# Batch 0's inverse on 32x32 blocks, its landmark sums made transposed, and a new order of all pieces, in a fused Nystrom-attention and SiLU-MLP kernel

## The chip, the cores and the metric

The kernel runs on one core of a Trainium2 chip. The metric is the device time of one execution in microseconds (us). Three runs of the kernel before gave 247.44, 250.91 and 253.49 us; the median, 250.91 us, is the time to compare with.

## The reference

Attention with landmarks (Nystromformer) over 8 batches of 8 heads, 576 tokens, head width 64, and then a two-layer network with SiLU on the joined heads. Per batch and head, with m = 32 landmarks that are means of 18 consecutive tokens:

```
q_lm, k_lm = means of 18 tokens                       # 32 x 64
A  = softmax(q k_lm^T / 8)      # 576 x 32
Bm = softmax(q_lm k_lm^T / 8)   # 32 x 32
C  = softmax(q_lm k^T / 8)      # 32 x 576
Z  = Bm^T / (norm1(Bm) * norminf(Bm))
six times: Z = 2 Z - Z Bm Z
attn = A Z C v                  # 576 x 64
out  = silu(x w_in) w_out       # x: 4608 x 512, w_in: 512 x 2048, w_out: 2048 x 512
```

All inputs and the output are float32; the kernel computes in bf16 and f16 with float32 sums.

## The kernel before

The work goes batch by batch, and the stages of neighbouring batches are interleaved. The eight heads of a batch are two groups g of four heads; a group's four 32-row blocks fill the 128 partitions. Per batch b:

- **Loads** (L360 to L425, queue of POOL, with the cast to bf16): `ld1.b` is k, `ld0.b` is q, `ldv0.b` to `ldv2.b` are v. Batch 0's q and k come as four halves (`ld00.0`, `ld01.0`, `ld11.0`, and the first half of k as float32 on SP's queue, `ldk`, cast on chip by `k0cACT` and `k0cDVE`). `wi..` are pieces of w_in, `wo..` of w_out. q and k lie in two buffers (batch b in buffer b mod 2), v too.
- **Transposes** of q and k: batches 0 to 2 on TensorE (`tr`, L512, evacuated by `trc`); batches 3 to 7 by four DMA transposes each on SP's queue (`xt10`, `xt11` for k, `xt00`, `xt01` for q, L539).
- **Landmark sums**: batches 0 and 1 on TensorE (`lms`, L555: 72 matmuls of 64 columns that add 18 slices each with the identity as weights; `lmc` copies the sums, `ltr`, L592, transposes them, `lmT` evacuates). From batch 2 on, a tree of additions on DVE (`lra` to `lrd`, L575), then `ltr` with the matrix `fold`, then `lmT`.
- **Bm and its inverse**: `sb` (L611), `pb` (exp), `pbs`, `pbr`, `bmx`, `csb`, `bmt`, `bbd`, `n1`, `nrm`, `f0`, `stz`, `stf`; then six steps. A step is `fb` (L683, a DVE product that spreads the 32x32 blocks of the weights into a block-diagonal 128x128 matrix), `ns` (L702, matmul) and `nsd` (L708, DVE: twice the state less the product). Batch 0 runs each group as a chain of its own (`ns00`, `ns01`, ...); the other batches run both groups together.
- **A, C and the rest**: `A`, `C` (matmuls), `Ax`, `Cx` (exp on ACT), `S`, `Ln`, `Rs`, `etn` (row sums and their division), `ct` (C transposed: `ctm` on TensorE for batches 0 and 1, a DMA transpose on SP at L814 after that), `cv` (C times v), `wc`, `zbd`, `zt`, and `m0` to `m3` (times w_in, evacuated by `mc`).
- **First layer** (L891): `h0` to `h15`, two matmuls of 512 columns each, and `hx`; ACT applies SiLU (`g`, `gx`).
- **Second layer**: `o` (plain products, the first ones) and from then on seven products `p1` to `p7` per pair of 128-row blocks, eight matmuls of 256 columns each, with sums on DVE (`ss`) and evacuations `c..`, `u2`; stores `os` on SP's queue, at the end on ACT's too.

`SEQUENCE` (L19) is one list of all these pieces, written out; each engine and each DMA queue runs its own pieces in the order of that list, and a piece starts when its operands are there. `*n` in it stands for n matmuls of 256 columns on zeros ("fillers", L442), which nothing reads. A name with `/ACT` or `/DVE` says which engine copies. Two rules add waits that the data don't ask for: a DMA transpose waits for one v load of its batch or of the next (`gate`, L539; L814), and the loads of a batch wait for the DMA transposes of an earlier one:

```
        gate = last[b - 1].get("xts", [])[-2:-1]
        if b - 2 >= NCT:
            gate = gate + last[b - 2]["cts"][:1]
        load_qk(b, 100.0 * b - 150, p["qk_read"], gate)
        load_v(b, 100.0 * b - 149, [p["cv"]], gate)
```

Of the kernel before, what the change touches and what calls it, by code (L numbers as in the profile page):

```python
# [19 lines left out]
ldk ld11.0 const ident k0cACT k0cDVE k0 *15 lms100.0 tr15.0 tr10.0 trc10.0/DVE lms106.0 lms1012.0  # L20
*6 lms110.0 lms116.0 tr114.0 lms1112.0 lmc1.0/DVE ld00.0 *6 lms000.0 tr05.0 tr00.0 trc05.0/ACT
trc114.0/ACT ltr1.0 lmT1.0/ACT trc00.0/DVE tr19.0 trc19.0/DVE trc15.0/DVE lms006.0 ld01.0
lms0012.0 lms010.0 lms016.0 lms0112.0 ld0.1 ld1.1 ldv2.0 ldv0.0 wi0b1 ldv1.0 wi0b0 tr09.0 tr014.0
lmc0.0/DVE *1 ltr0.0 lmT0.0/ACT *6 sb.0 pb.0 trc014.0/DVE trc09.0/DVE A.0 Ax01.0 Ax00.0 Ax10.0
Ax11.0 *5 C.0 Cx01.0 Cx10.0 Cx11.0 Cx00.0 pbs.0 pbr.0 bmx.0 bmt.0 csb.0 n1.0 nrm.0 tr09.1 lms000.1
lms006.1 S10.0 lms0012.1 lms010.1 bbd.0 trc09.1/DVE stz.0 f0.0 stf0.0 stf1.0 fb00.0 lms016.1
Ln10.0 S00.0 Ln00.0 fb01.0 lms0112.1 lmc0.1/DVE S01.0 ns00.0 nsd00.0 Ln01.0 S11.0 ns01.0 Ln11.0
nsd01.0 fb11.0 ctm00.0 ctc00.0/DVE tr05.1 trc05.1/ACT tr00.1 trc00.1/ACT Rs1.0 Rs0.0 ns11.0
nsd11.0 fb10.0 fb21.0 tr19.1 trc19.1/DVE ltr0.1 lms100.1 lms106.1 ns10.0 nsd10.0 lms1012.1 tr014.1
lms110.1 lms116.1 trc014.1/DVE ns21.0 tr114.1 lmT0.1/ACT wi1a wi0a wi1b1 wi1b0 wi3b0 wi3a  # L30
lms1112.1 lmc1.1/ACT tr10.1 trc10.1/ACT tr15.1 *2 ltr1.1 lmT1.1/ACT fb20.0 nsd21.0 etn1.0
trc15.1/DVE ns20.0 fb31.0 *3 ns31.0 ctm10.0 trc114.1/ACT etn0.0 nsd31.0 sb.1 pb.1 *1 A.1 Ax01.1
Ax00.1 nsd20.0 fb30.0 pbs.1 wrc.0 *1 ns30.0 nsd30.0 ctc10.0/DVE fb40.0 pbr.1 fb41.0 bmx.1 bmt.1
wi3b1 Ax11.1 Ax10.1 *5 C.1 Cx00.1 Cx11.1 Cx01.1 *1 ns40.0 nsd40.0 ns41.0 nsd41.0 fb50.0 fb51.0
cv0.0 cv1.0 wc.0 S01.1 Ln01.1 ns50.0 nsd50.0 *2 ns51.0 bbd.1 nsd51.0 zbd.0 S11.1 Ln11.1 S00.1
Ln00.1 wi2b0 wi2b1 wi2a ldv0.1 ldv1.1 *5 zt.0 ztc.0/DVE S10.1 ctm00.1 ctc00.1/DVE Rs0.1 Ln10.1
Cx10.1 *2 m1.0 mc11.0/ACT mc10.0/DVE m0.0 f0.1 mc01.0/DVE mc00.0/ACT *1 ctm10.1 ctc10.1/DVE Rs1.1
# [12 lines left out]
nrm.2 stz.2 o3@5000.0 hx8.1 f0.2 gx8.1 h0.1 g0.1 oc@5000.0/ACT h2.1 h10.1 g10.1 h4.1 h1.1 g2.1  # L50
g1.1 wt11 wt21 stf0.2 fb00.2 ns00.2 h13.1 g13.1 wt31 nsd00.2 fb10.2 wt10 wt20 wt30 p1@5020.0
c1@5020.0/ACT ns10.2 nsd10.2 fb20.2 h9.1 h6.1 g4.1 g9.1 g6.1 ss00@5100.0 p5@5020.0 c5@5020.0/DVE
hx0.1 gx0.1 ss10@5100.0 l1done.0 C.2 Cx00.2 Cx10.2 p6@5020.0 u2@5020.0/DVE ld1.3 ldv1.3 xt10.3
xt11.3 ns20.2 nsd20.2 ss20@5100.0 p3@5020.0 c12@5020.0 p7@5020.0 ld0.3 xt01.3 xt00.3 ldv0.2 ldv2.2
ldv1.2 l1done.1 A.2 Ax01.2 Cx11.2 ct1.2 Ax10.2 Ax11.2 p1@5100.0 c1@5100.0/ACT Ax00.2 Cx01.2 ct0.2
os@5000.0 ld1.4 lra1.3 fb30.2 ns30.2 p2@5020.0 ss30@5100.0 lrb1.3 os@5001.0 S10.2 S11.2 Ln11.2
Ln10.2 Rs1.2 p6@5100.0 S01.2 Ln01.2 S00.2 Ln00.2 p5@5100.0 nsd30.2 lrc1.3 fb40.2 lrd1.3 ltr1.3
c22@5020.0 lra0.3 u2@5100.0/DVE lrb0.3 p4@5020.0 ns40.2 lrc0.3 lrd0.3 ltr0.3 c11@5020.0 etn1.2
nsd40.2 c5@5100.0/ACT p3@5100.0 Rs0.2 lmT1.3/ACT etn0.2 lmT0.3/ACT sb.3 c12@5100.0 c21@5020.0/ACT
p7@5100.0 pb.3 pbs.3 pbr.3 fb50.2 A.3 Ax11.3 cv0.2 ldv1.4 c22@5100.0 wrc.2 wc.2 ld0.4 ldv0.3  # L60
ldv2.3 ldv2.4 ns50.2 nsd50.2 Ax10.3 Ax00.3 S11.3 Ln11.3 Ax01.3 p2@5100.0 C.3 Cx00.3 Cx01.3 Cx10.3
# [6 lines left out]
p4@5120.0 c21@5120.0/ACT nsd20.3 fb30.3 ns30.3 hx0.2 nsd30.3 fb40.3 h15.2 gx0.2 g15.2 ns40.3
nsd40.3 ct0.3 xt00.4 ld1.5 ldv0.4 h9.2 g9.2 g14.2 h1.2 h0.2 g1.2 g0.2 cv0.3 ldv1.5 fb50.3
ss30@5120.0 ns50.3 wc.3 nsd50.3 zbd.3 ld0.5 h11.2 g11.2 h13.2 g4.2 g13.2 h3.2 g3.2 etn1.3 zt.3  # L70
ztc.3/DVE etn0.3 p3@5120.0 c12@5120.0 m3.3 mc30.3/ACT m0.3 mc01.3/DVE mc00.3/ACT m2.3 mc21.3/ACT
m1.3 mc20.3/ACT h2.2 hx8.2 g2.2 h6.2 g6.2 mc31.3/DVE h12.3 gx8.2 h3.3 h10.3 mc10.3/DVE mc11.3/DVE
h7.3 h2.3 g2.3 h4.3 g4.3 g10.3 h13.3 h5.3 g5.3 hx8.3 gx8.3 g13.3 h9.3 h11.3 g7.3 h14.3 h6.3 g6.3
g11.3 p1@5200.0 g3.3 h8.3 g8.3 ss00@5200.0 p5@5200.0 hx0.3 g14.3 g9.3 ss00@5220.0 xt11.4 xt01.4
xt10.4 ss10@5200.0 lra1.4 lrb1.4 lrc1.4 ss10@5220.0 ss20@5220.0 lrd1.4 lra0.4 lrb0.4 os@5020.0
ss20@5200.0 l1done.2 ltr1.4 h1.3 h0.3 g0.3 g1.3 g12.3 h15.3 gx0.3 c1@5200.0/DVE p6@5200.0
u2@5200.0/ACT os@5021.0 ss30@5200.0 c5@5200.0/DVE p3@5200.0 ss30@5220.0 lmT1.4/DVE lrc0.4 lrd0.4
ltr0.4 lmT0.4/ACT g15.3 p1@5220.0 sb.4 pb.4 c1@5220.0/ACT xt11.5 xt10.5 c12@5200.0 lra1.5 lrb1.5
lrc1.5 p7@5200.0 c22@5200.0 lrd1.5 p2@5200.0 c11@5200.0 p4@5200.0 c21@5200.0/ACT C.4 Cx11.4 Cx10.4
Cx01.4 p6@5220.0 u2@5220.0/ACT Cx00.4 p5@5220.0 c5@5220.0/ACT A.4 Ax01.4 Ax10.4 Ax00.4 Ax11.4  # L80
pbs.4 pbr.4 bmx.4 xt01.5 xt00.5 lra0.5 csb.4 ss00@5300.0 p1@5300.0 S10.4 ltr1.5 p7@5220.0 lrb0.5
ss10@5300.0 ss20@5300.0 lrc0.5 n1.4 nrm.4 wrc.4 lrd0.5 ltr0.5 lmT0.5/ACT S00.4 p3@5220.0 l1done.3
os@5120.0 os@5121.0 Ln10.4 os@5200.0 ct0.4 ld0.6 stz.4 c1@5300.0/ACT bmt.4 lmT1.5/DVE bbd.4 f0.4
sb.5 pb.5 stf0.4 S11.4 Ln11.4 Rs1.4 p2@5220.0 S01.4 Ln01.4 fb00.4 ns00.4 c22@5220.0 pbs.5
c11@5220.0 c12@5220.0 Ln00.4 p5@5300.0 c5@5300.0/ACT Rs0.4 p4@5220.0 c21@5220.0/ACT pbr.5
# [96 lines left out]
class Plan:  # L182
# [14 lines left out]
    def run(self):  # L197
# [5 lines left out]
        seen = set()  # L203
# [41 lines left out]
def kernel(  # L245
# [9 lines left out]
    nc = tc.nc  # L255
# [907 lines left out]
```

## Time and profile before

| what | us |
|---|---|
| runs | 247.44, 250.91 (median), 253.49 |
| span of the profiled execution, first to last instruction | 245.4 |
| TensorE (PE) busy in it, fillers included | 233.3 |
| ACT, DVE, POOL busy | 180.8, 180.0, 36.7 |
| PE: first filler to first landmark sum | 1.13 to 5.00 |
| PE: longest idle stretch after that | 5.42 (98.75 to 104.17) |
| PE: granted clock of 0.50 | 101.54 to 108.37 |
| PE: last matmul ends | 241.0 |

The profiled execution's own time is its span and what lies around it; the page gives the span alone, which is 2.0 us below the fastest run and 5.5 below the median. A busy share is the union of an engine's instructions. Matmuls overlap, so the duration of one (193 ns for 64 columns) is longer than the distance to the next.

### The profile page before, as it was taken

What the parts mean: (1) busy time and instruction counts of PE and PEld (TensorE: products, weight loads), DVE (VectorE), ACT (ScalarE), POOL (GpSimd) and SP (SyncE); (2) the same over time, 40 slices, a digit from 0 to 9 for tenths busy, and PEclk for the clock granted to TensorE, in tenths of its full rate; (3) what the DMA queues carried; (4) which work ended last, traced back from release to release, by engine and by line L of the source; (5) the groups of instructions that cost most, each with busy time, mean ns of one, the idle gap of its engine ahead of it and who ended that gap; (6) DMA issues with size and microseconds to landing.
All of it is one profiled execution on the core that took longest, in us unless ns stands there. A gap on an engine that the chain in (4) does not pass through costs nothing.

```text
span 245.4 us, 7471 instructions
## 1 busy us (share of the span) xinstructions
PE 233.3 (95%) x2948; PEld 165.8 (68%) x2948; DVE 180.0 (73%) x503; ACT 180.8 (74%) x432; POOL 36.7 (15%) x62
## 2 busy tenths in 40 slices
PE   7999999999999999199999999999999999999992
PEld 5986464457867556067878754777876765789882
DVE  2589889789998591489798968938899475348752
ACT  3299999988989998159746699999779788634100
POOL 8346713000050040000130060000000000000000
PEclk9999999999999999769999999999999999999999
DMA  6999999999999999793999999985414421012343
GB/s 160 207 203 197 206 207 206 210 205 204 132 177 220 202 137 178 185 194 98 136 190 171 167 185 239 190 145 136 108 47 117 121 52 39 1 43 77 88 119 109
DMA packets 55876, 36.84 MB, mean 150 GB/s; under 512 B 36640, under 2 KB 47392, under 8 KB 55840
## 3 DMA queue, kind: packets, MB, share of 16 engines
q0 software_dynamic: 15120, 18.06, 45.1%
q1 hardware_dynamic: 39808, 17.35, 34.9%
q10 hardware_dynamic: 912, 0.95, 1.4%
q8 instruction: 23, 0.38, 0.6%
q14 instruction: 13, 0.11, 0.1%
HBM read 36.70 MB, written 9.44 MB: 188 GB/s over the span
## 4 chain that ended last, share of the span: by engine, by line
PE 78%; ACT 7%; DMA 7%; SPq 3%; issue 1%; DVE 1%; ACTq 0%; DVEq 0%
PE ps L325 74%; DMA qT<-qk 6%; PE ps L515 3%; SPq L539 2%; ACT gm L913 2%; DMA gm<-in_k_dram 1%; ACT L913 1%; SPq L814 1%; ACT L1116 1%; ACT gx L936 1%; ACT m L335 1%; PE ps L802 1%; DVE red L575 1%; ACT pb L641 1%; ACT et L742 0%
## 5 line engine op out<-in xcount | busy, mean ns | idle before, releaser
L913 ACT ACTIVATE gm<-ps 128x512 f16<-128x512 f32 x128 | 68.7, 621 | 15.0 <-PE ps L325 14.3
L325 PE MATMUL ps<-etn,m 128*128 128x512 bf16 (+1 forms) x512 | 73.5, 289 | 0.2
L325 PEld LDWEIGHTS <-gm 128*128 128x128 f16 x512 | 48.6, 98 | 12.5 <-issue 1.3
L325 PE MATMUL ps<-w_out_sb,gm 128*128 128x256 f16 (+1 forms) x392 | 53.0, 281 | 0.0
L325 PEld LDWEIGHTS <-ss 128*128 128x128 f16 x408 | 39.5, 99 | 9.8 <-issue 1.8
L325 PEld LDWEIGHTS <-m 128*128 128x128 bf16 x512 | 31.5, 98 | 20.8 <-issue 3.2
L325 PE MATMUL ps<-wt,ss 128*128 128x256 f16 x272 | 35.5, 276 | 0.2
L1036 DVE TENSOR_TENSOR ost<-ost,ps 128x256 f32<-128x256 f32 x51 | 20.9, 416 | 13.4 <-PE ps L325 7.4
L335 ACT COPY ost<-ps 128x256 f32<-128x256 f32 (+1 forms) x45 | 17.2, 388 | 10.9 <-PE ps L325 10.6
L335 ACT CAST m<-ps 128x512 bf16<-128x512 f32 x36 | 19.4, 612 | 1.1 <-PE ps L325 0.8
L337 DVE CAST m<-ps 128x512 bf16<-128x512 f32 x28 | 18.3, 685 | 2.3 <-PE ps L325 1.9
L710 DVE SCALAR_TENSOR_TENSOR st<-st,ps 128x128 bf16<-128x128 bf16 (+2 forms) x54 | 13.6, 257 | 8.5 <-PE ps L325 5.5
L407 POOL DMA_DIRECT2D v<-in_v_dram x24 | 14.0, 590 | 30.8 <-DMA qT<-qk 13.6
L325 PE MATMUL ps<-w_out_sb,ss 128*128 128x256 f16 x136 | 17.5, 273 | 0.0
L325 PE MATMUL ps<-wt,gm 128*128 128x256 f16 x120 | 15.5, 272 | 0.0
L575 DVE TENSOR_TENSOR red<-qT 128x1024 f16<-128x1024 bf16 x12 | 8.3, 689 | 9.4 <-DMA qT<-qk 9.2
L685 DVE TENSOR_TENSOR fb<-st,hmask 128x256 bf16<-128x256 bf16 (+1 forms) x54 | 14.4, 271 | 0.8
L752 ACT ACTIVATE ln<-ps 128x288 f32<-128x288 f32 x32 | 12.4, 423 | 2.7 <-PE ps L325 2.4
L787 ACT ACTIVATE ce<-ps 128x288 bf16<-128x288 f32 x32 | 13.0, 424 | 1.7 <-PE ps L325 1.6
L1001 DVE TENSOR_TENSOR ss<-gm 128x1024 f16<-128x1024 f16 x15 | 10.2, 686 | 5.2 <-ACT gm L913 5.2
L742 ACT ACTIVATE et<-ps 128x288 bf16<-128x288 f32 x32 | 11.1, 423 | 3.6 <-PE ps L325 3.6
L337 DVE COPY ost<-ps 128x256 f32<-128x256 f32 x25 | 10.5, 420 | 3.2 <-PE ps L325 3.0
(93 smaller groups left out, 332.0 us busy)
## 6 DMA issues: line engine op xcount, KB each, us to landing
out_dram<-ost SPq DMA_DIRECT2D x126, 64.0 KB, 2.1
v<-in_v_dram POOLq DMA_DIRECT2D x24, 192.0 KB, 10.0
qk<-in_q_dram POOLq DMA_DIRECT2D x7, 576.0 KB, 10.6
qk<-in_k_dram POOLq DMA_DIRECT2D x7, 576.0 KB, 9.2
w_out_sb<-in_moe_w_out_dram POOLq DMA_DIRECT2D x4, 512.0 KB, 15.1
w_in_sb<-in_moe_w_in_dram POOLq DMA_DIRECT2D x8, 128.0 KB, 7.2
w_in_sb<-in_moe_w_in_dram POOLq DMA_DIRECT2D x4, 256.0 KB, 9.0
out_dram<-ost ACTq DMA_DIRECT2D x10, 64.0 KB, 1.7
```

Of the source, the lines that this page charges most:

```text
L325: nc.tensor.matmul(out=out_ap, lhsT=lhsT, rhs=rhs, start=start, stop=stop, skip_group_check=True)
L335: nc.scalar.copy(out=out, in_=in_)
L337: nc.vector.tensor_copy(out=out, in_=in_)
L407: lambda e, a=a: nc.gpsimd.dma_start(out=v_r[b % 2][a * L:(a + 1) * L, :, :], in_=v[b].rearrange("h (l a x) d -> a l h (x d)", l=L, a=VA)[ ...
L575: lambda e: nc.vector.tensor_tensor(out=o_, in0=a_, in1=b_, op=OP.add),
L685: nc.vector.tensor_tensor(out=fb[it % 2][:, g0:g1], in0=bc(sr[it % 3][:, g0:g1, 0:L], 4, 2), in1=bc(hmask, n, 1), op=OP.mult), [o], 14.5 + ...
L710: nc.vector.scalar_tensor_tensor(out=s2[:, g0:g1, lo:SW], in0=s[:, g0:g1, lo:SW], scalar=2.0, in1=ps[:, 0:NG * SW].rearrange("p (g x) -> p ...
L742: lambda e, g=g, et=et, c=c: nc.scalar.activation(out=et[:, c], in_=bank(me["A"], 2 * g + c)[:, 0:HS], func=AF.Exp, scale=sc / J),
L752: lambda e, g=g, c=c, ln=ln: nc.scalar.activation(out=ln[:, c], in_=bank(me["S", g, c])[:, 0:HS], func=AF.Ln),
L787: nc.scalar.activation(out=ce[:, :, 0:VP].rearrange("p (i c) (a l) -> p c a i l", c=2, a=VA)[:, c], in_=bank(me["C"], 2 * g + c)[:, 0:HS]. ...
L913: lambda e, dc=dc, cell=cell: nc.scalar.activation(out=gm[:, dc, :], in_=bank(cell["o"]), func=AF.Silu),
L1036: nc.vector.tensor_tensor(out=out_, in0=x, in1=y, op=OP.add)
```

## The change

It does three things.

1. **Batch 0's landmark sums transposed.** The weights are now the 64 columns of a q or k slice and the moving operand is the 128-column identity, so the sum comes out transposed. It is made twice, into PSUM partitions 0 to 63 and 64 to 127, with two matmuls for each of the 72 slices: 144 matmuls of 128 columns in place of 72 of 64. `lmc` and `ltr` of batch 0 fall away; `lmT` reads the sums directly.
2. **Batch 0's inverse on compact blocks.** `ns` of batch 0 multiplies the 32x32 blocks as they lie, eight matmuls of 32 rows and 32 columns of weights per step (each block at its own quarter of rows and columns); `fb` falls away, and both groups run as one chain, like the other batches. 12 `ns`, 12 `nsd`, 12 `fb` and 2 `stf` become 6 `ns`, 6 `nsd` and 1 `stf`.
3. **A new `SEQUENCE`** for all pieces of all batches: 46 fillers in place of 64, and the waits between kinds of transfers are no longer made by rules but written in the list, as `name<other`: the piece waits until the transfer `other` has landed.

The core of the diff:

```
-            name, _, e = word.partition("/")
+            word, *gates = word.split("<")
+            name, _, e = word.partition("/")
             o = named.pop(name)
-            assert all(id(d) in seen for d, _ in o.deps), name
-            seen.add(id(o))
+            placed[name] = o
+            o.after = [placed[x] for x in gates]
...
-                    qt_ops[t, g][0].after = gate
...
                             for j in range(j0, j0 + 6):
+                                if cr:
+                                    for c in range(2):
+                                        mm(ps[Dh * c:Dh * c + Dh, g * 128:(g + 1) * 128],
+                                           qk[:, t, g, j, :], idb, start=(j == 0),
+                                           stop=(j == J - 1))
+                                    continue
                                 mm(ps[:, g * Dh:(g + 1) * Dh], idb, qk[:, t, g, j, :],
...
-        parts = [[0], [1]] if cr else [[0, 1]]
+        for gs in ([0, 1],):
...
                     for g in gs:
+                        if cr:
+                            for h in range(4):
+                                r = slice(L * h, L * h + L)
+                                mm(ps[r, g * SW + lo:(g + 1) * SW], s[r, g, 0:L], s[r, g, lo:SW])
+                            continue
                         mm(ps[:, g * SW + lo:(g + 1) * SW],
                            fb[it % 2][:, g].rearrange("p a l -> p (a l)"), s[:, g, lo:SW])
...
-                ct_ops[g][0].after = v_ops.get(b + 1, [])[-2:-1]
```

(`cr` is true for batch 0 alone.) The waits in the new list:

```
ld1.1<ldk ld0.1<ldk wi3a<ldk ldv1.0<ldk ldv0.0<ldk wi3b0<ldk ldv2.0<ldk
xt10.3<wo2 ldv1.3<xt11.3 ldv1.2<xt10.3 ldv2.2<xt01.3 xt00.3<ldv1.3 ct0.2<ldv1.2
ld1.4<os@5000.0 ldv2.3<ct1.2 ld1.5<xt11.4 ld0.5<xt10.4<os@5020.0 ldv1.5<xt00.5
ct1.4<ld0.7 ldv2.4<ct1.4 ldv1.4<ct1.4 ld0.6<os@5200.0 ld1.7<ct0.4 ldv2.7<xt00.6
ldv1.6<os@5341.0 ldv0.6<ct0.6 ldv1.7<ct0.6
```

The DMA pieces around batch 4's transposes, in the two lists (other pieces left out):

```
before: ct1.2 ct0.2 os@5000.0 ld1.4 os@5001.0 ldv1.4 ld0.4 ldv0.3 ldv2.3 ldv2.4 os@5100.0
        os@5101.0 ct1.3 ct0.3 xt00.4 ld1.5 ldv0.4 ldv1.5 ld0.5 xt11.4 xt01.4 xt10.4 os@5020.0
after:  ct1.2 os@5000.0 ldv0.2 ct0.2 ld1.4 os@5001.0 ldv2.3 ldv0.3 ld0.4 xt11.4 os@5021.0 ld1.5
        ct1.3 ct0.3 xt00.4 os@5020.0 xt10.4 xt01.4 os@5100.0 ld0.5 xt10.5 os@5121.0 xt11.5 xt00.5
        ldv1.5 xt01.5 ld0.7 os@5120.0 os@5101.0 ld1.6 os@5201.0 ct1.4 ldv2.4 ldv0.4 ldv1.4
```

Before the first `lms` the list has 15 fillers before and 8 after; from there to the first `h` 48 and 33; behind that 1 and 5. The loads of batch 0 start with q in the new list (`ld00.0 ld01.0`, then `ld11.0`), with k before.

More of the change, by code (lines that the diff above doesn't have):

```diff
@@ L19 @@
 SEQUENCE = """
[L20 to L25, printed above, removed]
@@ L32 @@
[L32 to L37, printed above, removed]
@@ L50 @@
[L50 to L61, printed above, removed]
@@ L68 @@
[L68 to L79, printed above, removed]
@@ L80 @@
[L80 to L85, printed above, removed]
@@ new lines @@
+trc15.2/ACT tr19.2 etn1.1 tr10.2 ns40.1 trc19.2/ACT trc10.2/DVE nsd40.1 *1 etn0.1 h14.0 g14.0 h8.0
+fb50.1 h5.0 g5.0 h13.0 tr114.2 h0.0 trc114.2/DVE lra1.2 lrb1.2 wrc.1 h4.0 l1done.3 g10.0 g3.0 g0.0
+g4.0 *1 ns50.1 nsd50.1 hx8.0 ld1.3 xt11.3 xt10.3<wo2 lrc1.2 zbd.1 gx8.0 lrd1.2 tr05.2 g13.0 g8.0
+trc05.2/DVE hx0.0 tr014.2 cv0.1 wc.1 tr00.2 wo3 ltr1.2 lmT1.2/ACT ld0.3 trc014.2/DVE zt.1 tr09.2
+ztc.1/ACT trc00.2/DVE h12.0 gx0.0 trc09.2/DVE g12.0 m3.1 mc30.1/ACT m2.1 m1.1 lra0.2 o0@5001.0
+mc20.1/DVE mc31.1/DVE lrb0.2 mc21.1/ACT o0@5000.0 h8.1 mc11.1/ACT lrc0.2 mc10.1/ACT h4.1 g4.1
@@ new lines @@
+S10.5 nsd50.4 wc.4 S11.5 zbd.4 Rs0.5 ct0.5 zt.4 c1@5340.0/ACT ztc.4/ACT xt10.6 ct1.5 c22@5320.0
+Ln10.5 xt11.6 nsd20.5 c12@5320.0 p4@5320.0 xt01.6 fb30.5 ns30.5 os@5301.0 Ln11.5 c21@5320.0/ACT
+nsd30.5 m1.4 m0.4 mc11.4/DVE m3.4 mc30.4/DVE p2@5340.0 p5@5340.0 mc31.4/ACT c11@5340.0 fb40.5
+ns40.5 xt00.6 Rs1.5 etn0.5 h14.4 mc00.4/DVE ss30@5340.0 mc10.4/ACT h7.4 g7.4 ss10@5340.0
+ld1.7<ct0.4 p6@5340.0 nsd40.5 fb50.5 c5@5340.0/ACT m2.4 p3@5340.0 mc21.4/ACT ns50.5 os@5321.0
+mc01.4/ACT u2@5340.0/DVE mc20.4/DVE g14.4 c12@5340.0 nsd50.5 ldv2.5 cv0.5 h15.4 g15.4 h12.4 h9.4
```

244 lines of the change are left out of this document (136 added, 108 removed).

## Prediction

> **What bounds the kernel now.** I read the page first, then the chain of waits, busy time by windows, and the timeline of the stretches that these name.
>
> ```profile
> span 245.4 us, 7471 instructions
> PE 233.3 (95%) x2948; PEld 165.8 (68%) x2948; DVE 180.0 (73%) x503; ACT 180.8 (74%) x432; POOL 36.7 (15%) x62
> PE   7999999999999999199999999999999999999992
> PEclk9999999999999999769999999999999999999999
> ```
>
> TensorE works all the time but for three places: the start, one hole at 40% of the span, where its clock falls too, and the end. The windows price them (columns: length, then busy time of PE, PEld, DVE, ACT, POOL, then granted clock, DMA share, GB/s).
>
> ```profile
> 1.13:5.00 3.87, 3.38 (x15) 2.25 (x16) 1.17 (x9) 1.68 (x2) 3.59 (x7) 1.00 0.70 194
> 31.25:98.75 67.50, 67.29 (x855) 42.64 (x853) 52.76 (x142) 62.73 (x143) 10.06 (x16) 1.00 1.15 189
> 98.75:104.17 5.42, 0.00 (x1) 0.00 (x1) 2.83 (x7) 0.44 (x1) 0.00 (x0) 0.76 0.74 182
> 104.17:108.40 4.23, 4.23 (x15) 2.10 (x16) 4.16 (x10) 2.06 (x4) 0.00 (x0) 0.51 1.07 201
> 108.40:241.00 132.60, 132.15 (x1566) 99.46 (x1563) 97.93 (x260) 93.24 (x227) 7.43 (x12) 1.00 0.60 119
> 241.00:245.40 4.40, 0.00 (x0) 0.00 (x0) 0.42 (x1) 0.00 (x0) 0.00 (x0) 0.94 0.30 81
> ```
>
> Outside the hole PE waits 0.21 us of 67.50 and 0.45 of 132.60. The chain (start, length, what) says what the hole is:
>
> ```profile
> 80.56 3.22 SPq L539
> ...
> 86.72 14.41 DMA qT<-qk
> ...
> 101.23 0.70 DVE red L575
> ...
> 104.17 15.06 PE ps L325 x139
> ```
>
> A DMA transpose of batch 4 is issued at 86.72 and lands 14.41 us later; the median of this kind is 4.2 (page, part 6). The sum tree on DVE and PE's `ltr1.4` wait for it. POOL shows what ran beside it:
>
> ```profile
> 86.34 0.71 POOL L400 DMA_DIRECT2D qk<-in_k_dram  x1 [13.68 <-issue]
> 87.04 1.16 POOL L407 DMA_DIRECT2D v<-in_v_dram  x2
> 88.20 0.71 POOL L400 DMA_DIRECT2D qk<-in_q_dram  x1
> ```
>
> The next batch's loads went out around that transpose. The start, in the timeline (start, length, instructions):
>
> ```profile
> 1.13 3.38 PE L325 MATMUL ps<-zer 128*128 128x256 bf16 x15 [1.13 <-DVE zer L434]
> 5.29 0.98 PE L515 MATMUL ps<-idb,qk 128*128 128x128 bf16 x9
> 6.46 0.82 PE L325 MATMUL ps<-zer 128*128 128x256 bf16 x6
> 8.69 0.67 PE L515 MATMUL ps<-idb,qk 128*128 128x128 bf16 x9
> 22.69 0.55 PE L325 MATMUL ps<-v,ct 96*32 96x64 bf16 x48
> ```
>
> Fifteen fillers take 0.21 us each, six later ones 0.11; nine transposes 0.98, later 0.67: PE is at half pace until about 6.2, though the clock column says 1.00 there.
>
> **The change, term by term**, against the span of 245.4.
>
> *The hole: -7.5.* It costs 5.42 idle, and then 4.23 us of work at clock 0.51, so 2.1 more. In the new list `xt11.4` no longer stands behind `ct1.3` and `ct0.3`, these two lose their wait for `ldv1.4`, and of the next batch's loads only `ld1.5` may run beside the last three transposes (`ld0.5` waits for `xt10.4`; `ldv1.5` for `xt00.5`). Between `xt01.4` and `ltr1.4` lie, in PE's order, 23 pieces `h`, 4 `hx`, 5 products and 5 `m`, about 18 us at 0.43 (42.74 to 43.17 in the timeline), 0.45, 0.87 (97.25 to 98.12) and 0.35; before, the last three transposes stood right ahead of their tree. Even the slowest landing, 14.4, then ends before `ltr1.4`. Bounds: 0 (the hole stays) to -7.5. I take -7.5, since what made the row of 14.41 late, two q/k loads and two v loads at once, is pulled apart.
>
> *Fillers: -1.2.* From the first landmark sum on 38 are left of 49, at 0.108. The first 15 becoming 8 gains nothing: PE waits for `ldk` either way (5.00).
>
> *`lmc`, `ltr` of batch 0: -0.2.* Four matmuls at 0.056 (nine transposes: 0.67 less one latency of 0.22, by 8). The two copies, 0.42 each, lie beside fillers and transposes; without these they would be 0.8 of path.
>
> *Landmark sums: +1.6.* Before, 72 at 0.034 (12 in 0.51), 2.4. After, 144 of 128 columns: 4.0 if the two halves overlap (72 x 0.056), 8.1 if not; so +1.6 to +5.7. I take +1.6, by the nearest row: 48 matmuls on column tiles in 0.55, or 8 ns each.
>
> *Newton steps: 0 on the path beyond the fillers.* DVE loses 12 `fb` (216 ns) and 12 `nsd` (212, two of 180), gains 6 of 283: 3.4 us less in a stretch, 12 to 27, where it is busy 13.16 of 14.95. The old chain runs from 15.51 (first `ns`) to 24.25 (`zbd`), 1.46 per step; a new step is 0.20 + 0.28 + two hand-overs of 0.1, 0.7, so 4.5 us less for six. But PE's order decides: between `sb.0` and `zt.0` it holds about as much other work as before, pulled up from batch 1. Bounds: -4.5 (the chain sets the start of `h`) to 0; I take 0, since PE idles 0.04 us there.
>
> *Tile changes: +1.4.* Sixteen 64x32 matmuls of `m` at 25.47 take 0.56 until the next piece starts, eight at 27.49 take 0.35: 0.026 each and 0.14 fixed. Ten new changes (6 `ns`, 4 groups of sums) cost 0 to 2.8 (in and out); I take one each, 1.4. The Trainium skill, TensorEngine Tiling (Array Packing), Key Properties, says that a change of the tiling mode drains TensorE; by it all changes in and out would pay, 2.8, and the sum would be 1.4 higher. The 0.14 agrees with it.
>
> *Clock at the start: +0.8.* Eight fillers end near 3.0, so PE now idles 2 us before `ldk` lands, not 0.5. If the half pace lasts 4.2 us from there, as after the hole, it ends at 9.2, not 6.2: 1.5 us lost; if not, 0. The middle, since the idle time lies between 0.5 and 5.42. The Trainium skill, TensorE: Matmul & The Clock Gate, Part 1, has the full clock granted after a busy window of about 3.4 us, in windows that run free; by it either end comes true from run to run. This run's 5 us until full pace doesn't contradict it.
>
> *Loads at the start: 0.* The order is q first, and PE's order follows; the bytes up to the last half are the same. `ident` stands behind two loads rather than one (0.55 us later, still 2 before `ldk`), so nothing is late. `wi1b1` and `wi2a`, the last of w_in, are issued as the last ones were at 22.97; `m1.0` and `m2.0` come about 1.5 earlier. Bounds 0 to +1.5; PE waited for none of them, so 0.
>
> *New waits elsewhere: +0.5.* Nearly every piece has moved. Bounds: 0 (0.66 us of waits in 200 us of the old order) and 7.5 (the hole). I take 0.5, near the many small rows.
>
> *The tail: 0.* Both lists end in the last evacuations and eight 32 KB stores; 4.40 stays.
>
> Sum: 245.4 - 7.5 - 1.2 - 0.2 + 1.6 + 1.4 + 0.8 + 0.5 = 240.8. What lies around the span is 2.0 (fastest run) to 5.5 (median); I take 3.5, as nothing says which run the profile resembles: **244.3 us**, 2.6% below the median of 250.91.
>
> **Rivals.**
>
> *A. v of batch 4 comes late (slower).* `ct1.4` waits for `ld0.7`, two v loads of batch 4 wait for `ct1.4`, and behind it on SP stand `ct0.4` and the stores. Walk with this run's median landings: `ld0.4` at 68 (it was 70.22) + 10.6; `xt00.4`, `os@5020.0` and `xt10.4` issue by 82.8, landing + 4.2 = 87; `ld0.5` + 10.6 = 97.6; `xt00.5`, `xt01.5` landed by 103.2; `ld0.7`, which overwrites what `xt01.5` reads, + 10.6 = 113.8; `ct1.4` + 3.9 = 117.7; v + 10.0 and two issues = 129. `cv0.4` was at 124.25, 116.8 without the hole; the new order has some 7 us of pieces more ahead of it, and the terms above 3 or 4: about 127. So by medians it is 2 us late; but after 100 us q/k landings were 4.3 and v 7.7 (median), and then v is there by 124. That speaks against it; the slowest v (12.1 there, 17.7 over all) speaks for it. It decides at 127, and makes the kernel slower than before once v lands after 131.5 (4.5 idle and 2.1 of half clock eat the 6.6 gained). With v at 133: 6 + 2.1 on 244.3, **252.4**.
>
> *B. The transposes are late all the same* (the change doesn't do what it says). `xt00.4`, `xt10.4`, `xt01.4` do run beside `ld1.5`, and `lra1.5` needs `xt10.5`, `xt11.5`, which start about 10 us before. A landing of 14.4 there stops DVE, in order, with `mc`, `ss` behind it, and PE after it. Price: the hole, +7.5: **251.8**.
>
> *C. The sums don't overlap.* +4.1 and, at half pace for the first half, 1 more: **249.4**. For it: 64 columns with a weight load per matmul is a shape that the trace lacks. Against: the column-tile row. The Trainium skill, TensorEngine Tiling (Array Packing), Restrictions, says that column tiling turns off Fast Weight Load; an estimate by the 53 ns per 64 columns of TensorE: Matmul & The Clock Gate (LDWEIGHTS) is 7.6 us for 144 loads in line, between my two ends, and 3.8 if pairs overlap.
>
> *D. Better.* The chain of batch 0 is what the old fillers waited for, and half of the 4.5 comes; no cold start (-0.8), no new wait: 244.3 - 3.5 = **240.8**.
>
> **How the numbers follow.** Forecast 0.50 (its own range 241 to 248: the clock, the tile changes and 2.0 to 5.5 around the span); A 0.15, B 0.13, C 0.08, D 0.14. Two per cent, about what a measurement of this kernel can tell from no change, is 5.0 us: 245.9 to 255.9. Faster than that: D and 0.36 of the forecast, 0.50. Within: 0.14 of the forecast, and 0.18 of A, B and C: 0.32. Slower: the other 0.18, where A, B or C cost more than put here or come together. The range 239 to 254.5 leaves out 0.1 at each end. Predicted: 244.3.
>
> **What would show it.** Right: no idle PE near `ltr1.4`, no granted clock of 0.5 in mid-run, a span near 241; `lms` of batch 0 within 4 to 5 us of PE, `ns` steps at 0.7 to 1.4. Wrong: PE idle ahead of the 96x64 matmuls of `cv0.4`, released by a DMA of v (A); DVE `red` released by `qT<-qk` for over 2 us (B); 64x128 matmuls 0.056 apart one by one (C).

## The result, and the profile after

The kernel after takes 253.87 us (median of 4 runs, 253.52 to 255.28), the kernel before 251.31 beside it (4 runs, 247.44 to 253.49): a ratio of 1.028, 95% interval 1.021 to 1.035. It is slower, where 244.3 was forecast. (The ratios here leave out runs more than 1.5% above the fastest of the same kernel; what is left of before lies near 247, so a ratio isn't the quotient of the medians.) What lies around the span is 1.7 us (253.5 less 251.8), so the profiled execution of before, with its span of 245.4, is like the fastest of its runs. Spans are compared from here on: 251.8 against 245.4, 6.4 more.

The page of the kernel after, the lines that were shown of before:

```profile
span 251.8 us, 7598 instructions
PE 236.5 (94%) x3034; PEld 166.3 (66%) x3034; DVE 175.3 (70%) x483; ACT 182.5 (72%) x431; POOL 36.7 (15%) x62
PE   4999999999999999795999999999999999999992
PEclk9999999999999999999799999999999999999998
```

The slice of before at 40% of the span, busy for one tenth, has become a 7. There is a second dent (5) two slices on, a low clock just after that, and a weaker start (4 for 7). The windows of after, cut at the first landmark sum, at 40 us, around the dent, and at the last matmul:

```profile
1.13:5.25 4.12, 1.88 (x8) 1.03 (x8) 1.69 (x13) 1.68 (x2) 2.55 (x5) 1.00 0.78 190
5.25:40.00 34.75, 33.58 (x626) 23.91 (x627) 19.80 (x61) 26.12 (x66) 17.88 (x28) 1.00 1.17 196
40.00:101.85 61.85, 61.28 (x780) 38.70 (x778) 50.41 (x136) 55.15 (x127) 6.33 (x10) 1.00 1.05 174
101.85:119.14 17.29, 12.90 (x137) 9.43 (x136) 12.31 (x28) 10.63 (x25) 2.01 (x3) 1.00 1.03 204
119.14:124.00 4.86, 4.86 (x43) 3.15 (x43) 3.52 (x10) 2.51 (x11) 0.38 (x1) 0.65 0.71 156
124.00:246.97 122.97, 121.95 (x1446) 90.12 (x1444) 86.90 (x236) 86.06 (x202) 7.38 (x13) 1.00 0.57 111
```

From the first landmark sum to the last matmul, the length less the busy time, plus the clock lost, comes to 1.17 + 0.57 + 4.39 + 1.70 (4.86 at 0.65) + 1.02 = 8.85 us. Before, it was 0.05 (5 to 40 us) + 0.21 + 5.42 + 2.1 + 0.45 = 8.2. So the hole went, and as much came back elsewhere. The rest of the 6.4 us is work: PE's busy time in that stretch, clock losses taken off, is 5.1 longer (232.9 against 227.8); batch 0's pieces and the fillers are the only work that changed. The tail adds 0.4 (4.83) and the later first sum 0.25.

The large waits of after in the timeline, PE first and then ACT:

```profile
103.32 1.04 PE L328 MATMUL ps<-etn,m 128*128 128x512 bf16 x4 [1.47 <-DVE m L340]
119.14 1.25 PE L328 MATMUL ps<-w_out_sb,ss 128*128 128x256 f16 x8 [2.92 <-ACT ost L338]
```
```profile
118.72 0.37 ACT L338 COPY ost<-ps 128x256 f32<-128x256 f32 x1 [3.66 <-DMA out_dram<-ost]
```

Read backwards: PE waits for a free PSUM bank, ACT for a free output tile (`ost`, six of them), and that tile for its store to DRAM. The chain of waits and SP's timeline have that store and what stood ahead of it:

```profile
111.06 7.58 DMA out_dram<-ost
```
```profile
103.01 4.15 SPq L533 DMA_TRANSPOSE qT<-qk  x3
107.26 8.12 SPq L984 DMA_DIRECT2D out_dram<-ost  x12
```

The store was issued at 111.06 and landed 7.6 us later (the median is 2.1), beside a q and a k load issued at 109.7 and 110.5; it is one of 12 stores that SP sent from 107.3 on, behind three transposes from 103.0 on.

The start of after:

```profile
5.25 2.13 PE L328 MATMUL ps<-idb,qk 128*64 128x128 bf16 x36 [2.24 <-ACT qk L338]
7.31 1.14 PE L509 MATMUL ps<-idb,qk 128*128 128x128 bf16 x9
8.62 2.12 PE L328 MATMUL ps<-idb,qk 128*64 128x128 bf16 x36 [0.16 <-DMA qk<-in_q_dram]
10.67 0.90 PE L509 MATMUL ps<-idb,qk 128*128 128x128 bf16 x13
11.50 1.20 PE L328 MATMUL ps<-idb,qk 128*64 128x128 bf16 x36
```

By the starts of these groups, 18 pairs of sums take 2.06 us in the first two and 1.12 in the third: 0.114 a pair, then 0.062. One matmul of 128 columns was put at 0.056 by the transposes of before, so pairs do overlap (C is out), but PE is at half pace until about 10.7, though the clock column says 1.00. All 72 pairs took 6.35 us, where the 72 sums of before took 2.2. Later there are waits laid to "issue", that is to nothing that the profile shows:

```profile
21.96 0.22 PE L509 MATMUL ps<-idb,qk 128*128 128x128 bf16 x1 [0.32 <-issue]
27.74 0.38 PE L328 MATMUL ps<-v,ct 96*32 96x64 bf16 x27 [0.41 <-issue]
```

### The profile page after: what moved, and what is told of

It is laid out like the page before. It is cut to its first block, busy times and chain, and to the rows that moved or that the text cites. A ratio compares the mean times of both kernels' runs of the same rounds, so it can differ in the third digit from the quotient of the medians.

```text
span 251.8 us, 7598 instructions
## 1 busy us (share of the span) xinstructions
PE 236.5 (94%) x3034; PEld 166.3 (66%) x3034; DVE 175.3 (70%) x483; ACT 182.5 (72%) x431; POOL 36.7 (15%) x62
## 4 chain that ended last, share of the span: by engine, by line
PE 66%; ACT 16%; DMA 8%; SPq 4%; issue 2%; DVE 2%; ACTq 0%; DVEq 0%; POOLq 0%
PE ps L328 63%; ACT gm L919 9%; DMA out_dram<-ost 5%; DMA qk<-in_q_dram 3%; SPq L984 2%; ACT m L338 2%; PE ps L509 2%; SPq L533 2%; ACT L919 1%; ACT gx L942 1%; PE ps L809 1%; ACT ost L338 1%; ACT L1122 1%; ACT ln L763 0%; DVE ost L1042 0%
## 5 line engine op out<-in xcount | busy, mean ns | idle before, releaser
L328 PE MATMUL ps<-etn,m 128*128 128x512 bf16 (+1 forms) x512 | 71.8, 286 | 2.3 <-DVE m L340 1.5
L328 PE MATMUL ps<-w_out_sb,gm 128*128 128x256 f16 (+1 forms) x392 | 54.6, 285 | 0.0
L328 PEld LDWEIGHTS <-ss 128*128 128x128 f16 x408 | 38.3, 98 | 10.6 <-issue 4.9
L328 PE MATMUL ps<-wt,ss 128*128 128x256 f16 x272 | 34.5, 273 | 0.0
L717 DVE SCALAR_TENSOR_TENSOR st<-st,ps 128x128 bf16<-128x128 bf16 (+1 forms) x48 | 13.0, 272 | 7.0 <-PE ps L328 6.6
L340 DVE COPY qT<-ps 128x512 bf16<-128x512 bf16 (+1 forms) x16 | 6.8, 453 | 9.2 <-PE ps L509 8.7
L686 DVE TENSOR_TENSOR fb<-st,hmask 128x256 bf16<-128x256 bf16 x42 | 11.9, 289 | 0.9
L942 ACT ACTIVATE gx<-ps 128x512 f16<-128x512 f32 x16 | 10.2, 661 | 2.8 <-PE ps L328 2.7
```

Source lines behind the costliest of these rows:

```text
L328: nc.tensor.matmul(out=out_ap, lhsT=lhsT, rhs=rhs, start=start, stop=stop, skip_group_check=True)
L340: nc.vector.tensor_copy(out=out, in_=in_)
L686: nc.vector.tensor_tensor(out=fb[it % 2][:, g0:g1], in0=bc(sr[it % 3][:, g0:g1, 0:L], 4, 2), in1=bc(hmask, n, 1), op=OP.mult), [o], 14.5 + ...
L717: nc.vector.scalar_tensor_tensor(out=s2[:, g0:g1, lo:SW], in0=s[:, g0:g1, lo:SW], scalar=2.0, in1=ps[:, 0:NG * SW].rearrange("p (g x) -> p ...
L942: lambda e, d0=d0, cell=cell, c=c: nc.scalar.activation(out=gx[:, d0:d0 + 8, c:c + 64], in_=bank(cell["o"]).rearrange("p (c x) -> p c x", ...
```

## The experiments

Two theories to begin with. One: the new code of batch 0 costs more than was put (sums, clock), and the list's gain is lost at the start. The other: the new list brings waits of its own, on other transfers, that are worth the old hole.

**Code and list apart.** The old list with its old waits and the new code of both parts; only the words of pieces that no longer exist are struck out:

```
-lmc0.0 lmc1.0 ltr0.0 ltr1.0 stf1.0 fb00.0 fb01.0 ns01.0 nsd01.0
...
```

> The old list of pieces with the old rules for the waits, but batch 0's landmark sums transposed and its inverse on compact blocks (the pieces that fall away are struck from the list, nothing else moves; all 64 fillers stay). Theory 1 (the new order with its waits costs the time, batch 0's new code little): within 2 us of the kernel before in the same call, 249 to 253. Theory 2 (batch 0's new code costs it, by the doubled sums and the tile changes): 4 us or more slower, 255 or above.

250.42 us, within the range of theory 1, but the ratio is 1.013 (1.004 to 1.022); span 248.4. The hole is still there but shorter (104.30 to 106.48, 2.18). The first up-projection (`h`) starts at 31.8 instead of 26.97: nearly 5 us late there, 3.0 at the end of the span, since the hole takes up some. The new code costs time by itself, between the two theories.

The old list with the compact inverse alone; of the words above, `lmc` and `ltr` stay, and the sums are the old ones:

```
-                                if cr:
+                                if LT:
                                     for c in range(2):
```

> The old list and its old waits with the compact inverse of batch 0 alone; the landmark sums stay as before (lmc and ltr included), all 64 fillers stay. Theory 1 (the doubled sums at half clock are what the new code costs at the start, some 4 us by the first h; the inverse costs 0 to 0.8 by its tile changes): within 1.5 us of the kernel before, and 1 to 3 below the run that has both. Theory 2 (the inverse's tile changes cost the 5 us): 250 or above, like the run that has both.

253.57 us, ratio 1.017 (1.005 to 1.029): theory 1, which put this kernel below the one with both parts, missed. The first `h` starts at 30.4, with a wait of 1.63 us on "issue" at 26.06, ahead of plain fillers. That wait had no place in either theory.

The new list with the old sums, and the new list with all old code (the inverse not split); the words that these need come in again:

```
-lms0112.0 lmT0.0/ACT tr09.0
+lms0112.0 lmc0.0/ACT tr09.0 ltr0.0 lmT0.0/ACT
...
-nsd10.0
+nsd10.0 fb20.0
```

> The changed kernel with the landmark sums of batch 0 made as before (72 matmuls of 64 columns, lmc, ltr put back into the new list ahead of lmT); the compact inverse and the new list with its waits stay. Theory 1: the start gains 3 to 4 us; what of it is left at the end depends on the holes between transfers, so 249.5 to 252.5. If the new order alone costs the time, 253 to 255.

> The list and gates of after with the code of before for batch 0 (sums of 64 columns with copy and transposition, Newton steps on spread blocks; those not split in halves): the order alone. Theory that the list gives back its own gain in other transfer waits: first up-projection at 27 to 29 us, but 4 to 8 us of holes over 1 us behind 40 us, span 246 to 252. Rival (the code of batch 0 is all that costs): no hole over 1.5 us behind 40 us, span 240 to 244.

253.51 and 254.16 us, three of four runs of each between 253.4 and 255.2, the fourth 248.53 and 250.00; no ratio was formed. The execution traced with all old code took 254.01 us. There the list alone still has 2.90 us of wait at 79, 1.36 at 118.6 and 1.68 at 130.5, and its first `h` is as late as with the new code (32.36):

```profile
81.84 0.28 PE L326 MATMUL ps<-zbd,wsb 128*128 128x128 bf16 x2 [2.90 <-DVE wsb L850]
```

So the list has its own late start and, in that execution, its own holes; "the code is all that costs" is out. What the list costs in its quickest executions isn't settled by one run of each.

**More warm-up.** After, with seven more fillers ahead of the first sum:

```
-l1done.2 wi0b0 lms100.0
+l1done.2 wi0b0 *7 lms100.0
```

> The changed kernel with 15 fillers ahead of the first landmark sum, as before the change, in place of 8; nothing else is altered. If the late full clock at the start costs what the trace shows (half pace to about 11.5 us instead of 6.1, some 2.5 us), the time falls by 1.5 to 2.5 us against the changed kernel's 253.9, to 251.4 to 252.4. If the early work only waits for loads anyway, it stays at 253.9 within 0.7.

255.50 us, ratio 1.026 (1.007 to 1.045), so no gain that these runs can tell. The first `h` starts at 31.6, 0.6 earlier, though the second group of sums is now at full pace (1.13 us for 18 pairs, from 8.44). The cold clock isn't the only bound of the start.

**The program's fetch.** In seven traces that stood before this test PE waits on "issue" at the same count of matmuls, behind the 351st or the 479th that the trace records or behind both, whatever stands there: fillers, transposes, C times v. (The expectations below count some more: 363 and 490.) The page's list of DMA queues has two of the kind "instruction"; the larger has 24 packets, 0.39 MB, in after: 3034 matmuls and as many weight loads make 253 instructions a packet. The theory is that PE takes its program in such blocks of some 128 matmuls, and that a block can't come quickly while the loads fill the DMA engines. To test it, before with each of its 63 early fillers issued as three of a third of the columns:

```
-  lambda e: mm(banks[7][:, 0:256], zer[:, 0:128], zer)
+  lambda e: mm(banks[7][:, 0:86], zer[:, 0:128], zer[:, 0:86])
```

> The kernel before, with each of the 63 fillers ahead of the first up-projection (one matmul of 256 columns) issued as three of 86 columns: the same columns, 126 more matmuls. Theory of the program fetch (in the traces so far TensorE takes about 127 matmuls, with their weight loads one 16 KB packet of its instruction queue, per 5 to 6.5 us while the loads run, and idles 'issue' near its 363rd and its 490th matmul, whatever these are): the first up-projection is then the 622nd matmul instead of the 496th and starts at 31 to 33 us (26.97 before), with an idle stretch laid to issue near the 363rd or 490th. Rival (the start is bound by TensorE's columns and its clock): first up-projection at 26.5 to 28 us. The whole time: fetch +1 to +5 us, rival within 1 us.

Every idle stretch laid to issue in that trace:

```profile
12.68 0.43 PE L329 MATMUL ps<-qT,lmT 64*32 64x288 bf16 x15 [0.42 <-issue]
18.88 0.25 PE L329 MATMUL ps<-qk,idb 128*128 128x64 bf16 x3 [0.91 <-issue]
25.07 0.31 PE L329 MATMUL ps<-qT,lmT 64*32 64x288 bf16 x5 [1.08 <-issue]
31.37 0.25 PE L329 MATMUL ps<-zer 128*128 128x86 bf16 x2 [1.70 <-issue]
```

They end 6.20, 6.19 and 6.30 us apart, behind 223, 351, 479 and 607 recorded matmuls, 128 apart each time, and between the first and the last the instruction queue moved three packets:

```profile
q0 software_dynamic: 3871, 3.67, 121.2%
q8 instruction: 3, 0.05, 1.0%
```

The first `h` starts at 31.46, 4.5 us later, for the same columns. The theory holds for the blocks: in this stretch PE gets one packet per 6.2 us, 49 ns for a matmul with its weight load (the two waits of after, 128 matmuls apart too, end 5.78 us apart, and before, with 468 matmuls from 5 to 26.9 us, 47 ns each, has no such wait). That the loads set this pace is argued, not shown: no run takes them away. The Trainium skill, Runtime: NRT & Kernel Launch, "Instruction fetch mechanics", has a refill in 16 KiB blocks of 256 instructions and calls it mostly hidden; the packets agree, the hiding fails here. The whole kernel loses only 0.9% (ratio 1.009, 1.003 to 1.015): the hole ahead of `ltr1.4` is 4.46 us in this trace, not 5.42, so a part of the late start is made up there.

After with half the columns in the landmark sums, and so half the sum left out, but as many matmuls:

```
-  mm(ps[Dh * c:Dh * c + Dh, g * 128:(g + 1) * 128],
-     qk[:, t, g, j, :], idb, start=(j == 0),
+  n = 64 if j else 128
+  mm(ps[Dh * c:Dh * c + Dh, g * 128:g * 128 + n],
+     qk[:, t, g, j, :], idb[:, 0:n], start=(j == 0),
```

> The kernel after, with the landmark sums of batch 0 streaming 64 columns instead of 128 in all matmuls but the first of each sum (the other half of the sums is left out): as many matmuls, half the columns. Fetch theory: first up-projection still at 31 to 32.5 us (32.26 in after), since the number of matmuls ahead of it is the same. Rival (array time and clock): the four stretches of the sums fall from 6.35 to about 3.3 us and the first up-projection comes at 29 to 30 us.

251.97 us, ratio 1.016 (1.004 to 1.027). First `h` at 31.27, with waits on issue of 0.58, 1.25 and 0.68 at the counts 223, 351 and 479. The sums fell from 6.35 to 3.7 us; the first `h` comes only 1.0 earlier, and the waits on issue are 1.8 longer than in after. Most of what the columns saved, the fetch took. Then fewer matmuls: sums of two neighbouring positions at a time in full-width weights, copied and folded, 36 in place of 144:

```
+  if j % 2 == 0:
+      mm(ps[:, g * 128:(g + 1) * 128], qk[:, t, g, j:j + 2, :].rearrange("p j d -> p (j d)"),
+         idb, start=(j == 0), stop=(j == J - 2))
```

> The kernel after, with the landmark sums of batch 0 made of two positions at a time (full 128x128 weights, 36 matmuls in place of 144), copied and then folded by one matmul a tensor: 106 matmuls fewer, about 0.7 us of copy and fold more on the path. Fetch theory: the first up-projection is about the 514th matmul and starts at 27 to 28.5 us (32.26 in after). Rival (the sums cost their time in the array at the clock granted): sums fall from 6.35 to 2.1 to 4.1 us, less the 0.7: first up-projection at 29 to 31.5 us. The end moves less than the start, since the holes behind move: span 246 to 252.

No wait on issue is left, and yet the first `h` starts at 30.51, not 27 to 28.5: a miss of the fetch theory as the only bound, in the range of its rival, the cold array (252.95 us, ratio 1.017, 1.003 to 1.030). With seven more fillers as well:

> The kernel after with the sums in pairs (106 matmuls fewer) and seven more fillers ahead of the first sum. Two bounds theory (a cold clock until about 11.5 us, and 6.2 us per 256 instructions behind it; either alone gave only 1.8 and 0.6 us since the other took over): first up-projection at 27 to 29 us, against 32.3 in after, 30.5 with pairs alone and 31.6 with the fillers alone. Rival (something else of the list holds up the start, such as the order of batch 0's casts and loads): 29.5 to 31 us. Span 244 to 251, since the list's holes behind 70 us stay.

First `h` at 30.53 (253.61 us, ratio 1.008, 1.000 to 1.016). The rival holds: something else of the list keeps the start late. The trace shows two parts of it. One is a load, and the clock behind it; PE's row, then the windows from there:

```profile
7.66 0.92 PE L325 MATMUL ps<-idb,qk 128*128 128x128 bf16 x9 [1.48 <-DMA qk<-in_q_dram]
```
```profile
7.66:9.00 1.34, 1.34 (x15) 1.34 (x16) 0.00 (x0) 0.00 (x0) 0.75 (x2) 0.60 1.09 194
9.00:11.50 2.50, 2.50 (x26) 2.40 (x24) 0.00 (x0) 0.96 (x2) 1.30 (x2) 0.53 1.10 206
```

With more warm-up PE is ready sooner, waits 1.48 us for a load of q, and then works 3.8 us at about half clock; the kernels of this list with the old sums wait for that load too, 1.16 and 1.41 us. The other part is the order. The first Newton step of this kernel, and of before:

```profile
21.05 0.24 PE L325 MATMUL ps<-st 32*32 32x64 bf16 x8
```
```profile
15.51 0.20 PE L325 MATMUL ps<-st,fb 128*128 128x64 bf16 x1
```

The new list has batch 1's sums, transposes and scores ahead of it. PE is busy with them, so this part of the lateness is work pulled forward and not time lost. That makes the first `h` a poor measure of loss: a kernel below has it at 32.59 and a span of 244.7, though three quarters of most of its stores are left out.

**The new holes.** The 27 waits struck out of the new list:

```
-ld1.5<xt11.4 ld0.5<xt10.4<os@5020.0 ct1.4<ld0.7
+ld1.5 ld0.5 ct1.4
...
```

> The changed kernel without any of the 27 written waits between transfers; only the data's own dependences stay. Theory 1a (the written waits delay the loads: POOL stood 10 to 18 us several times): faster, 249 to 252. Theory 1b (they keep transposes, loads and stores apart and the order of the other pieces costs the time): slower or unchanged, 254 to 258.

274.28 us (268.29 to 278.24): holes of 9.20, 7.08 and 4.24 us, each with a spell of half clock. The written waits protect; they aren't what costs. Next the two loads beside the late store put behind the stores:

```
-xt01.5 ld0.7 os@5120.0 os@5101.0 ld1.6 ct1.4<ld0.7
+xt01.5 os@5120.0 os@5101.0 ld0.7<os@5101.0 ld1.6 ct1.4
```

> The changed kernel; the two loads of q and k that went out at 109.7 and 110.5 us (ld0.7, ld1.6) wait for the store os@5101.0 and stand behind it in the list, and ct1.4 no longer waits for ld0.7. If the 2.92 us that PE stood at 116.2 (an evacuation that waits for an output buffer whose store took 7.6 us beside these loads) and the half clock behind it (1.7 us) are the loads' doing, that hole goes: 2 to 4.6 us less than the changed kernel, 249.3 to 251.9. If the stores are late because the transposes stand ahead of them on SP's queue, nothing is gained: 253 to 255.

Ratio 1.028 (1.017 to 1.038). The hole at 116 is gone; one of 2.82 us at 126.6 (laid to ACT's `ln`), with a clock of 0.63 over the 4.58 us behind it, takes its place. Then only a quarter of each store up to the last batch (the other three quarters of the output's rows are left out):

```
-  [store(e, t, places[h], m) for m in range(4)]
+  [store(e, t, places[h], m) for m in range(1)]
```

> The kernel after with one store of four left out of none but the tail's: of each finished 128x512 piece of the second layer only the first of its four stores is made until the last batch (the other three quarters of these rows are left out). Theory: the hole at 116 (2.92 us, with the half clock behind it) and those near 78 and 126 of the other kernels with this list come of output tiles whose stores land late, behind SP's transposes and beside loads. Then there is no idle stretch over 1 us laid to ost, wsb or ln between 70 and 135, and the span falls from 251.8 to 246 to 248; the one near 102 (m, behind the transposes) stays. Rival (each hole taken away gives way to the next transfer, as with the loads behind the stores): one of 2 us or more stays between 70 and 135, span 250 or more.

246.21 us, ratio 0.994 (0.990 to 0.998), span 244.7. The stretch from 101 to 135 us, in after and in this kernel:

```profile
101.00:135.00 34.00, 29.22 (x314) 21.73 (x312) 24.88 (x69) 21.65 (x63) 6.33 (x10) 0.95 0.95 184
```
```profile
101.00:135.00 34.00, 34.00 (x427) 26.94 (x425) 29.27 (x90) 25.35 (x74) 6.34 (x10) 1.00 0.89 158
```

PE doesn't idle at all, at full clock, and behind 40 us no wait is over 0.51. PE's last matmul ends 6.84 us earlier than in after, though this start is worse (1.80 and 0.68 on issue). Even the wait at 102, which was expected to stay, is gone. The stores, with what hangs on them, are the new holes. The run takes away their packets on the DMA engines and their places on SP's queue at once, and doesn't tell these apart.

Are they late for their place on SP? After with the stores moved up in the list to 12 words behind the last write of their piece (25 of 30 move, most ahead of transposes), and the same with the pair sums; one of the moves, some 175 words, with only the transfers shown:

```
-xt10.4 xt01.4 ld0.5 xt10.5 os@5121.0 xt11.5 xt00.5 ldv1.5 xt01.5 ld0.7 os@5120.0 os@5101.0
+os@5101.0 xt10.4 xt01.4 ld0.5 xt10.5 os@5121.0 xt11.5 xt00.5 ldv1.5 xt01.5 ld0.7 os@5120.0
```

> The kernel after, complete, with each store of a finished output piece moved up in the list to 12 words behind the last instruction that writes the piece (25 of 30 stores move, most of them ahead of transposes and loads on SP and POOL). If late stores make the holes behind 70 us, and their place behind SP's transposes makes them late, the holes laid to ost, wsb and ln near 78, 116 and 126 go and the span falls from 251.8 to 245 to 248, near the 244.7 with a quarter of the stores. Rival 1 (the stores are slow for the loads that share the DMA engines, wherever they stand): the holes stay, span 249 to 253. Rival 2 (a store that waits for its piece now holds up the transposes behind it on SP): a hole of 2 us or more laid to red, rs or ct.

> The kernel after with the sums in pairs and the stores early: 106 matmuls fewer and the holes of the stores gone, if both theories hold. Span 241 to 246, ratio to before 0.965 to 0.985. Rival (transposes or loads pay for the stores, or the start stays as late and costs as much): span 247 or more.

260.80 and 254.65 us, ratios 1.050 (1.025 to 1.075) and 1.028 (0.985 to 1.072). The waits on output tiles are gone, and a larger one has come, on a transpose of `ct`. PE's row in the first of the two, then SP's:

```profile
95.66 0.83 PE L324 MATMUL ps<-v,ct 96*32 96x64 bf16 x48 [6.18 <-DMA ct<-ce]
```
```profile
81.22 6.26 SPq L980 DMA_DIRECT2D out_dram<-ost  x11
87.59 2.87 SPq L817 DMA_TRANSPOSE ct<-ce  x2
```

Eleven stores stand ahead of that transpose now. Rival 2 of the expectation is right: on one queue, in order, what is taken from the stores is paid by the transposes.

**The old hole, alone.** Before, with batch 5's loads (`ld1.5`, `ldv1.5`, `ld0.5`, whose words move along) behind `xt10.4`, the last of batch 4's transposes on SP, where the rule had picked `xt00.4`, the first:

```
-        gate = last[b - 1].get("xts", [])[-2:-1]
+        xts = last[b - 1].get("xts", [])
+        gate = xts[:1] if b == 5 else xts[-2:-1]
```

> The kernel before with one wait moved: the loads of batch 5 (q, k and v) wait for xt10.4, the last of batch 4's four transposes on SP's queue, instead of xt00.4, which is the first there, and ld1.5, ldv1.5, ld0.5 stand behind xt10.4 in the list. If the hole of 5.4 us and the half clock behind it come from those loads beside the transposes, it goes: 4 to 7.5 us less than the kernel before in the same call. If the transposes are slow by themselves, or the later loads make another hole, it stays within 2 us.

245.01 us, ratio 0.986 (0.975 to 0.996), span 242.6, and no low clock in mid-run:

```profile
PE   7999999999999989979999999999999999999992
PEclk9999999999999999999999999999999999999999
```
```profile
109.48 1.03 PE L322 MATMUL ps<-wt,gm 128*128 128x256 f16 x8 [2.06 <-DVE ost L1033]
```

The wait at `ltr1.4` is gone; this one of 2.06 us has come, behind a wait of DVE for a transpose (2.40 us), and one of 1.19 at 86.4. One wait in the right place gets about what the whole new list was forecast to get (244.3); of all complete kernels here this is the fastest. Three more built on it: with the compact inverse; with fewer instructions at the start (fillers joined in twos, pair sums); with early stores.

> The old list with the compact inverse alone and with batch 5's loads behind xt10.4, as in the first run of this call. If both gains add: as that run or up to 1 us less, 241 to 245. If the inverse brings nothing: as that run.

> The best kernel so far (the old list with batch 5's loads behind the last transpose) with fewer instructions at the start: fillers ahead of the first up-projection joined two and two to 512 columns (31 fewer), and batch 0's landmark sums in pairs with a fold (36 fewer). If the fetch of the program bounds the old start too, the first up-projection comes 1.5 to 3 us earlier than with the gate alone (27.8 us) and the ratio to before falls from 0.986 to 0.975 to 0.982. Rival (the old start stays just under that bound, and the chain of the Newton steps sets it): 27 to 28 us, ratio 0.983 to 0.99.

> The old list with batch 5's loads behind the last transpose, and each store moved up in the same way (stores there stand up to 212 words behind their piece). If late stores cost the old list too: the hole of 2.06 us at 107 and the one of 1.19 us at 86 go, ratio to before 0.970 to 0.982. Rival (there the stores fill gaps of SP and the transposes pay for the move): ratio 0.985 to 1.0, with a hole laid to the transposes.

The first: 250.82 us, ratio 1.004 (0.998 to 1.011), a miss of both its expectations: the compact inverse takes back what the gate gave. The second: 253.94 us (one run of 246.46, the others above 253), no ratio; its first `h` starts at 26.91 against 27.81, so the rival is about right and the old start is hardly bound by the fetch, though a wait of 0.46 on issue stands behind matmul 351. Both traces show a new hole near 154 (4.16 and 5.05 us), laid to the sums behind batch 6's transposes; they are of executions of 252.30 and 254.66 us, and the quickest of the two kernels, 247.81 and 246.46, were not traced. The third: 280.80 us, ratio 1.134 (1.115 to 1.154), holes of 7.16 and 5.16 us behind transposes; the old list pays for early stores more than the new one.

## Why the prediction was wrong, step by step

- **The hole, -7.5: right.** No idle PE near `ltr1.4` (it ran at 107.74 without a wait), the low clock there gone. The gate kernel, with batch 5's loads kept off batch 4's transposes and nothing else changed, confirms the cause.
- **New waits elsewhere, +0.5: the step that failed.** Waits and lost clock behind 40 us measured 7.7 (0.57 + 4.39 + 1.70 + 1.02). The old order's own 0.66 was part of the 245.4, so the term came to 7.0, close to its upper bound of 7.5 and not to 0.5. The prediction took its value "near the many small rows" of the old order, though "nearly every piece has moved"; one order that had few waits says little on another. The cause of the largest wait, a store that holds an output tile, stood in no rival. A followed v and `ct1.4`, and PE didn't wait at batch 4's C times v. B was there in small, by its own sign (more than 2 us of DVE): DVE waited 2.94 and 0.72 us for batch 4's transposes near 95 to 99, which ends in the 1.47 at 103.

```profile
97.02 0.69 DVE L577 TENSOR_TENSOR red<-qT 128x1024 f16<-128x1024 bf16 x1 [2.94 <-DMA qT<-qk]
```

- **Landmark sums, +1.6, and clock, +0.8: mis-sized.** The sums measured +4.2 (6.35 against 2.2). All at the warm price of 0.062 a pair (put at 0.056) they would be +2.3; half of the pairs, cold at 0.114, add 1.9, which belongs to the clock term. The full pace came 5.4 us behind PE's restart at 5.25, at about 10.7, not 6.2 or 9.2; the 4.2 taken from behind the hole was too short. The Trainium skill, TensorE: Matmul & The Clock Gate, Part 1, gives about 3.4 us of busy time; these two kernels took 5.0 (before, from 1.13 on) and 5.4. With the same 15 fillers as before, other traces had the full pace by 5.1 (the compact inverse alone) and only near 9.5 (all new code in the old list), so the clock's part differs from trace to trace.
- **Fillers -1.2, `lmc` and `ltr` -0.2, tile changes +1.4, Newton 0.** With the sums and the clock they were to come to +2.4; PE's busy time rose by 5.1. What is left beside the sums and the fillers, about 2.1, is the half pace of the other pieces and the tile changes, which weren't taken apart. "Newton 0" counted columns and chains; the compact inverse alone and the fillers in thirds show what was missing, a price per instruction: 49 ns a matmul in this stretch, for 36 more of them in the six steps. In after itself it shows as only 0.7 us of waits (0.32 and 0.41); with seven more fillers they are 1.1, so it seems that the cold clock had held PE below the fetch.
- **The tail, 0, and 3.5 around the span.** The tail came to +0.4. Around the span lie 1.7, so that term was 1.8 too high and by luck hides a part of the error: the sum for the span was 11.0 too low (240.8 against 251.8), the time 9.6. Loads at the start, 0, came to 0.16 in after; it is the quicker starts above that wait for q.

The forecast of a faster kernel thus fell by about 7 us of new waits and 4 us of start. What the code of batch 0 costs at the end is not settled: 3.0 us of span in the old list (one trace each), where the hole takes up a part.

## What to carry to other kernels

When an order is changed as a whole, price the waits of the new one at the hole that the old one had, not at the old one's quiet stretches: stores, transposes and loads share engines and queues here, and closing a hole by moving one of them often opened another (116 to 126 us; output tiles to `ct`). Before rewriting an order, try the one wait that the trace names. And count instructions as well as columns wherever many small matmuls run beside heavy loads.

## What the runs showed of the hardware beside that

At the start, while the loads moved about 200 GB/s, packets of PE's program came 6.2 us apart in the trace with fillers in thirds, 49 ns for a matmul with its weight load. Thirteen of the twenty traces have waits on "issue" in the first 36 us, and all stand behind 223, 351, 479 or 607 recorded matmuls. A matmul on a 128x64 column tile that streams 128 columns costs 0.062 us a pair warm, so the two halves do run side by side, and 0.114 at half pace. A store of 64 KB lands in 2.1 us by the median and in 7.6 beside two 576 KB loads. And a hole of 2.92 us was enough for the clock to fall: 0.65 granted over the 4.86 us that follow; one of 2.44 (the pair sums, 0.57 over 3.77 us) was enough too, one of 2.06 (the gate kernel) wasn't.
